# Eleven stores of decoded token weights move from ScalarE's DMA queue to SyncE's in a fused attention and two-mixer kernel

## The chip, the cores and the metric

The kernel runs on one core of one Trainium2 chip. The metric is the device time of one execution in microseconds (us). The kernel before was run three times; the median is 758.35 us, the runs lie between 756.17 and 761.12 us. Beside these stands one profiled execution, of which every row below is taken.

Engines are called as in the profile: PE is TensorE's matmul side and PEld its weight load, DVE is VectorE, ACT is ScalarE, POOL is GpSimd, SP is SyncE, which computes nothing and issues most of the DMAs. A name with a q (SPq, ACTq) is an engine's sequencer, which issues DMAs.

## The reference

Eight batches of 576 tokens, model width 512, all in float32. The steps, cut to what matters here:

```
kv  = einsum('bhsd,bhse->bhde', k, v);  out = einsum('bhsd,bhde->bhse', q, kv)
x   = out / sqrt(mean(out*out) + 1e-6) * g_norm           # heads side by side: (8, 576, 512)
gate = sigmoid(causal 5-tap depthwise conv of x);  val = x @ w_val
y   = (gate * val) @ w_out                                # end of the first stage
theta = y @ w_theta;  zr, zi = y*cos(theta), y*sin(theta)
u   = y + w_tok_r @ zr + w_tok_i @ zi                     # mixing over the tokens
result = u + relu(u @ w_ch)
```

Some weights arrive as 64-bit floats, two 32-bit words for each number, and the kernel turns them into float32 itself. w_tok_r and w_tok_i (called w_tok together) are 9 x 576 columns of 128 rows. They are needed only in the second stage, where u is made.

## The kernel before, in words

**Two stages.** The first stage (about the first 310 us) makes attention, the gated value product and w_out's product for one batch after the other, in a loop over i = 0..7 (line 392). It writes its result y of each batch to a DRAM buffer (`ydram`). The second stage (from line 445 on) reads y back, makes theta, the mixing over tokens and the channel product, and writes the result. Every product is done as three matmuls on a high part and a low part of each operand (`parts`, line 66: ACT copies the high part, DVE subtracts to get the low part).

**An iteration of the first stage.** PE makes the value products v of batch i, then w_out's products y of batch i, and between them the attention of batch i + 2: `key_value` (kvp, line 182), the products o with q (line 200), the sums of squares ss (line 212). DVE makes the gating (`acc`, line 288), the low parts (line 69), the convolution of the next batch (line 265), the inverse roots (lines 219 to 225) and the scaling of x by them (line 246). ACT makes high parts, squares, sigmoids (line 266) and the copies of y out of PSUM (yo, line 304), which it then stores itself on its own queue (`yd<-yo`, line 305).

**SP's queue in an iteration.** In the order of the trace: the inverse roots go to DRAM and come back broadcast (`rd<-y`, line 228, and two `yb<-rd`, line 233); then the next keys and values in eight loads (`kv`, lines 156 and 157), then the next q in four loads (line 168), then loads of raw weights (`raw_tk`, `raw_wt`, line 85).

**The decoding of chunks beside it.** Lines 430 to 441 run in iterations 1 to 6. Each of them takes one 512-wide chunk of w_theta (four in all) and three of w_tok (eleven in all, the last 64 wide). A chunk is loaded by SP (`fetch`, line 71, tile `raw_tk` or `raw_wt`, three buffers shared), decoded by four DVE operations and one of ACT (`decode`, line 88: DVE lines 94, 95, 96, ACT line 97, DVE line 98) into a tile `dst_tk` or `dst_wt`, **two buffers shared by both kinds**. A w_theta chunk is then split into parts that stay in SBUF (ACT line 112, DVE line 113). A w_tok chunk is stored to DRAM, into `tokdram` (`td<-dst_tk`, line 441), from where the second stage reads it (line 551). As the two buffers are shared, the first operation of a later chunk (line 94) must wait until the buffer's earlier content was read: by line 113, or by the DMA of line 441, until that has landed.

**What sets the order.** The text gives an order, but not the one that runs. A planner works out, before the run, the order of the instructions on each engine from estimated durations: at each time it takes, of the instructions whose inputs and buffers are there by its estimate, the one that stands first in urgency, and each engine then works off its list strictly in order. The block of lines 430 to 441 stands under `tc.high_priority(offset=-LATER)` with LATER = 1000, so that all of it, the loads, the decoding and the stores, counts as a thousand places less urgent than where it stands in the text. The waits are made from the data and buffers that are used. In iterations of the trace the chunks' decoding stands between the convolution's operations on DVE. [...]

**Names in the steps below.** The iteration of the trace that is called the third runs from the row `rd<-y` at 156.25 us to the one at 195.20 us, the fourth from there to 234.81 us, the fifth from there to 271.10 us, the second from 124.28 to 156.25 us. The f loads (line 330) are the first loads of the second stage; they go into the space that the raw and dst tiles had.

Of the kernel before, what the change touches and what calls it, by code (L numbers as in the profile page):

```python
# [43 lines left out]
def attention_moe_holo_kernel(ctx, tc, kvm, kvt, qt, gn, w_val, conv_w, w_out, w_th, w_tok, w_ch, outT):  # L44
# [5 lines left out]
    nc = tc.nc  # L50
# [37 lines left out]
    def decode(pool, raw, width, name, tag=""):  # L88

        if raw.dtype == F32:  # L90
            return raw
        dst = pool.tile([P, width if tag else DM], F32, tag="dst" + tag if pool is px else "fTt", bufs=(1 if tag else 2) if pool is px else 1, name=f"dst_{name}")[:, :width]
        lo, hi, d = raw[:, :width, 0], raw[:, :width, 1], dst.bitcast(I32)
        nc.vector.tensor_scalar(d, hi, 0x07FFFFFF, 3, ALU.bitwise_and, ALU.logical_shift_left)
        nc.vector.scalar_tensor_tensor(d, hi, -0x40000000, d, ALU.bitwise_and, ALU.bitwise_or)
        nc.vector.scalar_tensor_tensor(d, lo, 29, d, ALU.logical_shift_right, ALU.bitwise_or)
        nc.scalar.activation(hi.bitcast(F32), hi.bitcast(F32), AF.Square)
        nc.vector.scalar_tensor_tensor(dst, hi.bitcast(F32), TINY, dst, ALU.is_ge, ALU.mult)
        return dst
# [4 lines left out]
    def weight_chunk(pool, tiles, src, k, name, scale=None, raw=None):  # L104
        h, l = tiles
        if raw is None:
            raw = fetch(pool, src[:, k, :], DM, f"{name}_{k}")
        st = decode(pool, raw, DM, f"{name}_{k}")
        if scale is None:
            parts(h[:, k, :], l[:, k, :], st)  # L110
        else:
            nc.scalar.activation(h[:, k, :], st, AF.Copy, scale=scale)
            nc.vector.scalar_tensor_tensor(l[:, k, :], st, scale, h[:, k, :].bitcast(F32), ALU.mult, ALU.subtract)
# [14 lines left out]
    tokdram = dr.tile([P, 9 * S], F32, tag="td", name="td")  # L128
# [3 lines left out]
    px = px_stack.enter_context(tc.tile_pool(name="px", bufs=1, reuse_waits="tile", side="right"))  # L132
# [18 lines left out]
    def load_kv(b, pairs=range(NP)):  # L151
        kv = []
        for p in pairs:
            t = px.tile([P, 2, 5, P], F32, tag="kv", bufs=4, name=f"kv{b}_{p}")
            nc.gpsimd.memset(t[D:P, :, 4, :], 0.0)
            nc.sync.dma_start(out=t[:, :, 0:4, :], in_=kvm[b, p])
            nc.sync.dma_start(out=t[0:D, :, 4, :], in_=kvt[b, p])
            kv.append(t)
        return kv
# [11 lines left out]
    def key_value(b, kv):  # L171

        ps = one_bank(f"kvp{b}")
        for g in range(2):
            for e in range(2):
                es = slice(e * D, (e + 1) * D)
                at = slice((2 * g + e) * D, (2 * g + e + 1) * D)
                for c in range(5):
                    for j in range(2):

                        t = kv[2 * g + j]
                        nc.tensor.matmul(ps[j * D:(j + 1) * D, at], t[:, 0, c, es], t[:, 1, c, es],
                                         start=(c == 0), stop=(c == 4), tile_position=(0, j * D))
        kvs_of[b] = pa.tile([P, NP, D], F32, tag="kvs", bufs=2, name=f"kvs{b}")
        nc.scalar.activation(kvs_of[b], ps[:, 0:NP * D].rearrange("p (a e) -> p a e", e=D), AF.Copy)
# [92 lines left out]
    def value(b, x, xh, xl, sg, between):  # L278
        gh = pa.tile([P, NM, S], F32R, tag="gh", bufs=1, name=f"gh{b}")
        gl = pa.tile([P, NM, S], F32R, tag="gl", bufs=1, name=f"gl{b}")  # L280
        for m in range(NM):
            between(m)
            g = sg[m]
            ps = two_banks(f"v{b}_{m}")
            for h in range(2):
                product(ps[:, h], wv, m, xh, xl, h * HS)
            halves = lambda t: t.rearrange("p (h s) -> p h s", h=2)
            nc.vector.tensor_tensor(halves(g), ps, halves(g), ALU.mult)  # L288
            last, _ = parts(gh[:, m, :], gl[:, m, :], g)
            if m + EARLY < NM:  # L290
                sg.append(conv(b, m + EARLY, x))
        return gh, gl, last
# [34 lines left out]
    def load_y(b):  # L327
        f = qx.tile([P, NM, S], F32, tag="full", bufs=2, name=f"f{b}")
        for m in range(NM):
            nc.sync.dma_start(out=f[:, m, :], in_=ydram[b][:, m, :])  # L330
        for h in range(2):
            sl = slice(h * 256, (h + 1) * 256)
            to_tokens(sdram[b][sl, :], [(f[:, :, sl], (0, 256))], "fT", 2, f"fT{b}_{h}")
        yh = qx.tile([P, NM, DM], F32R, tag="yh", bufs=1, name=f"yh{b}")
        yl = qx.tile([P, NM, DM], F32R, tag="yl", bufs=1, name=f"yl{b}")
        for m in range(NM):
            parts(yh[:, m, :], yl[:, m, :], f[:, m, :DM])
        yt = qx.tile([P, 4, DM], F32, tag="yt", bufs=1, name=f"yt{b}")
        nc.sync.dma_start(out=yt, in_=sdram[b].rearrange("(c p) d -> p c d", p=P))
        return f, yh, yl, yt  # L340

    def load_tails(b):

        ft = qx.tile([P, NM, 2, D], F32, tag="ft", bufs=1, name=f"ft{b}")
        for j in range(2):
            nc.sync.dma_start(out=ft[:, :, j, :], in_=ydram[b + j][:, :, DM:S])
        to_tokens(stdram[b // 2], [(ft[:, :, j, :], (2 * j, D)) for j in range(2)], "fTt", 1, f"fTt{b}")
        th = qx.tile([P, NM, P], F32R, tag="th", bufs=1, name=f"th{b}")
        tl = qx.tile([P, NM, P], F32R, tag="tl", bufs=1, name=f"tl{b}")
        parts(th, tl, ft.rearrange("p m j s -> p m (j s)"))  # L350
        yts = []
        for j in range(2):
            t = qx.tile([P, S], F32, tag="tok", bufs=2, name=f"ytt{b}_{j}")[:, :DM]
            for r in range(2):
                nc.sync.dma_start(out=t[r * D:(r + 1) * D], in_=stdram[b // 2][j * D:(j + 1) * D, :])
            yts.append(t)
        return th, tl, yts
# [4 lines left out]
    raw = {}  # L362
# [29 lines left out]
    for i in range(B):  # L392
        if i == B - 1:
            px_stack.close()
            qx = ctx.enter_context(tc.tile_pool(name="qx", bufs=1, reuse_waits="tile", side="right"))
            ys = load_y(0)
            tls = load_tails(0)
            for k in range(CHFIRST):
                weight_chunk(qx, wch, w_ch, k, "wc")
        two = i + 2 < B  # L400
        if two:
            ahead = attention(i + 2, qs.pop(i + 2))

        def between(m):

            if two and m == 1:
                key_value(i + 2, kvs.pop(i + 2))
                if i + 3 < B:
                    kvs[i + 3] = load_kv(i + 3)
            if two and m == 3:  # L410
                next(ahead)

        gs = value(i, *xs, sg, between)
        if two:
            next(ahead)
            if i + 3 < B:
                qs[i + 3] = load_q(i + 3)
        if i + 1 < B:
            with tc.issue_after(gs[2].ins):
                *_, (nxs, last) = normalize(i + 1, *xy)  # L420
        if i == 0:
            for k in range(4):
                weight_chunk(px, wo, w_out, k, "wo", raw=raw[f"o{k}"])
        got = []
        first(i, *gs[:2], lambda: got.append(next(ahead) if two else None))
        xy = got[-1]
        if i + 1 < B:
            xs = nxs
            sg = [conv(i + 1, m, xs[0]) for m in range(EARLY)]
        if 1 <= i < B - 1:  # L430
            with tc.high_priority(offset=-LATER), tc.issue_after(last.ins):
                for _ in range(RATE[0]):
                    if todo:
                        w, src, k, name, scale = todo.pop(0)
                        weight_chunk(px, w, src, k, name, scale)
                for _ in range(RATE[1]):
                    if toks:
                        j = toks.pop(0)
                        sl = slice(j * DM, min((j + 1) * DM, 9 * S))
                        raw = fetch(px, w_tok[:, sl], sl.stop - sl.start, f"tk_{j}")  # L440
                        nc.scalar.dma_start(out=tokdram[:, sl], in_=decode(px, raw, sl.stop - sl.start, f"tk_{j}"))

# [111 lines left out]
    for b in range(B):  # L556
        f, zs = nxt
# [53 lines left out]
```

## Time and profile before

| | |
|---|---|
| median of 3 runs | 758.35 us (756.17 to 761.12) |
| time of the profiled execution | 757.05 us |
| its span, first to last instruction | 755.3 us |
| mean granted PE clock | 0.980 |
| DMA issues of line 441 | 11, 326 to 362 ns each on ACT's sequencer |
| from their issue to landing | 2.5 to 8.5 us, median 5.4 us |
| bytes of one such store | 256 KB (10 of them), 32 KB (the last) |
| DMA packets of ACT's queue, share of the 16 engines | 12.09 MB, 4.3% |
| DMA packets of SP's queue, share of the 16 engines | 89.75 MB, 42.3% |

The page of the profile gives, in this order: the busy time of each engine, the span in 40 slices, the DMA queues, the chain of work that ended last followed back from the last instruction, the groups of instructions, and the DMA issues. In the view of waits a row names the engine and line that waited, who released it, and then the sum in us, the number of times and the longest. In the view by windows each row is a stretch of the span: its length, then busy us and instruction count of each engine, the granted PE clock, the DMA share and GB/s. In the timeline a row begins with start and duration in us; brackets at the end hold the idle time before it and its releaser.

### The profile page before, as it was taken

How to read it: one execution, taken by the hardware profiler on the slowest of the kernel's cores; microseconds unless marked ns; L12 is line 12 of the kernel's file. 1: busy time of each engine (PE TensorE's matmuls, PEld its weight loads, DVE VectorE, ACT ScalarE, POOL GpSimd, SP SyncE). 2: the span in 40 equal slices, each digit the busy share in tenths (PEclk: the TensorE clock that was granted, in tenths of full speed). 3: DMA queues.
4: the chain of work that ended last, by engine and by line, in shares of the span. 5: the costliest groups of instructions: out<-in, count | busy, mean ns of one | idle time of the engine just before them, and what ended most of it. 6: DMA issues, size and time to landing. Idle time of an engine off the chain costs nothing.

```text
span 755.3 us, 14663 instructions
## 1 busy us (share of the span) xinstructions
PE 713.3 (94%) x6000; PEld 672.7 (89%) x6000; DVE 524.2 (69%) x930; ACT 337.6 (45%) x560; POOL 19.5 (3%) x72
## 2 busy tenths in 40 slices
PE   1679999998979899999999999999999999999998
PEld 1568989996969899889899899899999999998998
DVE  5389959978879999789883863853853934936504
ACT  2466565736364736376541641621732513614301
POOL 4000000000000000000000000000000000000000
PEclk9779999998989999999999999999999999999999
DMA  9949694978575257724336034063052160160101
GB/s 263 280 147 243 195 242 133 270 244 243 162 243 168 67 159 231 221 66 137 123 100 194 1 126 112 18 170 107 17 151 71 61 184 37 57 176 7 63 1 63
DMA packets 77058, 104.87 MB, mean 139 GB/s; under 512 B 11712, under 2 KB 42560, under 8 KB 76992
## 3 DMA queue, kind: packets, MB, share of 16 engines
q1 hardware_dynamic: 70224, 89.75, 42.3%
q10 hardware_dynamic: 6192, 12.09, 4.3%
q0 software_dynamic: 576, 2.10, 0.9%
q8 instruction: 47, 0.77, 0.4%
q14 instruction: 19, 0.16, 0.1%
HBM read 72.73 MB, written 31.19 MB: 138 GB/s over the span
## 4 chain that ended last, share of the span: by engine, by line
PE 64%; DVE 22%; ACT 6%; DMA 5%; issue 2%; SPq 0%; ACTq 0%; DVEq 0%
PE u L514 10%; PE u L512 10%; PE u L513 10%; DVE acc L265 9%; PE c L276 4%; PE c L275 4%; PE c L274 4%; PE th L460 3%; PE th L459 3%; PE th L458 3%; DMA td<-dst_tk 3%; DMA kv<-in_kvm_dram 2%; DVE xl L69 2%; DVE acc L288 2%; DVE gl L69 2%
## 5 line engine op out<-in xcount | busy, mean ns | idle before, releaser
L517 DVE TENSOR_TENSOR f<-u,f 128x288 f32<-128x288 f32 x64 | 26.5, 454 | 129.4 <-PE u L514 129.4
L265 DVE SCALAR_TENSOR_TENSOR acc<-x,cw,acc 128x576 f32<-128x576 f32 x128 | 101.9, 813 | 0.9 <-ACT acc L263 0.8
L68 ACT ACTIVATE uh<-f 128x288 fp32r<-128x288 f32 x64 | 26.2, 444 | 152.0 <-DVE f L517 152.0
L274 PE MATMUL y<-gh,woh 128*128 128x288 f32 x256 | 78.7, 308 | 2.9 <-DVE acc L288 1.7
L274 PE MATMUL v<-xh,wvh 128*128 128x288 f32 x256 | 77.7, 304 | 0.0
L276 PE MATMUL y<-gl,woh 128*128 128x288 f32 x256 | 76.8, 302 | 0.3 <-DVE gl L69 0.3
L275 PE MATMUL y<-gh,wol 128*128 128x288 f32 x256 | 77.0, 301 | 0.0
L276 PE MATMUL v<-xl,wvh 128*128 128x288 f32 x256 | 76.5, 299 | 0.0
L275 PE MATMUL v<-xh,wvl 128*128 128x288 f32 x256 | 76.1, 297 | 0.0
L274 PE MATMUL c<-uh,wch 128*128 128x288 f32 x256 | 75.4, 295 | 0.0
L276 PE MATMUL c<-ul,wch 128*128 128x288 f32 x256 | 75.4, 295 | 0.0
L275 PE MATMUL c<-uh,wcl 128*128 128x288 f32 x256 | 75.4, 294 | 0.0
L274 PEld LDWEIGHTS y<-gh,woh 128*128 128x128 f32 x256 | 49.9, 195 | 7.2 <-ACT x L205 3.1
L274 PEld LDWEIGHTS v<-xh,wvh 128*128 128x128 f32 x256 | 48.7, 190 | 3.9 <-issue 2.1
L460 PE MATMUL th<-wth,yl 128*128 128x512 f32 x128 | 50.3, 393 | 0.0
L459 PE MATMUL th<-wtl,yh 128*128 128x512 f32 x128 | 50.0, 391 | 0.0
L276 PEld LDWEIGHTS y<-gl,woh 128*128 128x128 f32 x256 | 49.6, 194 | 0.5 <-DVE gl L69 0.5
L458 PE MATMUL th<-wth,yh 128*128 128x512 f32 x128 | 50.0, 391 | 0.0
L275 PEld LDWEIGHTS y<-gh,wol 128*128 128x128 f32 x256 | 49.8, 195 | 0.0
L276 PEld LDWEIGHTS v<-xl,wvh 128*128 128x128 f32 x256 | 48.6, 190 | 0.3 <-issue 0.2
L275 PEld LDWEIGHTS v<-xh,wvl 128*128 128x128 f32 x256 | 48.8, 190 | 0.0
L275 PEld LDWEIGHTS c<-uh,wcl 128*128 128x128 f32 x256 | 48.0, 188 | 0.3
(188 smaller groups left out, 1946.4 us busy)
## 6 DMA issues: line engine op xcount, KB each, us to landing
kv<-in_kvm_dram SPq DMA_DIRECT2D x32, 512.0 KB, 9.1
q<-in_qt_dram SPq DMA_DIRECT2D x32, 288.0 KB, 7.0
yd<-yo ACTq DMA_DIRECT2D x32, 288.0 KB, 2.1
f<-yd SPq DMA_DIRECT2D x32, 288.0 KB, 4.0
out_dram<-f SPq DMA_DIRECT2D x64, 144.0 KB, 1.8
sd<-fT SPq DMA_DIRECT2D x64, 128.0 KB, 2.5
yt<-sd SPq DMA_DIRECT2D x8, 1024.0 KB, 5.4
yb<-rd SPq DMA_DIRECT2D x12, 576.0 KB, 7.0
```

What stands on the lines that cost most here:

```text
L69: return nc.vector.tensor_tensor(l, src, h.bitcast(F32), ALU.subtract), one
L265: nc.vector.scalar_tensor_tensor(a, x[:, m, k:k + S], cw[:, m * 5 + k:m * 5 + k + 1], a, ALU.mult, ALU.add)
L274: nc.tensor.matmul(ps, wh[:, m, ks], xh[:, k, tsl], start=(k == 0), stop=False)
L275: nc.tensor.matmul(ps, wl[:, m, ks], xh[:, k, tsl], start=False, stop=False)
L276: nc.tensor.matmul(ps, wh[:, m, ks], xl[:, k, tsl], start=False, stop=(k == 3))
L458: nc.tensor.matmul(ps, yh[:, k, :], wth[0][:, k, :], start=(k == 0), stop=False)
L459: nc.tensor.matmul(ps, yh[:, k, :], wth[1][:, k, :], start=False, stop=False)
L460: nc.tensor.matmul(ps, yl[:, k, :], wth[0][:, k, :], start=False, stop=(k == 3))
L512: nc.tensor.matmul(ps[:, :HS], zh[:, ms], wkh[:, j, sl], start=(i == 0), stop=False)
L513: nc.tensor.matmul(ps[:, :HS], zh[:, ms], wkl[:, j, sl], start=False, stop=False)
L514: nc.tensor.matmul(ps[:, :HS], zl[:, ms], wkh[:, j, sl], start=False, stop=(i == 8))
L517: nc.vector.tensor_tensor(f[:, m, sl], ps[:, :HS], f[:, m, sl], ALU.add)
```

## The change

Line 441 issues the store of a decoded w_tok chunk on SP's queue and not on ACT's. The stores of the w_out results (line 305) stay on ACT's queue. Nothing else is edited; the planner makes its order anew from the changed text.

```diff
                         raw = fetch(px, w_tok[:, sl], sl.stop - sl.start, f"tk_{j}")
-                        nc.scalar.dma_start(out=tokdram[:, sl], in_=decode(px, raw, sl.stop - sl.start, f"tk_{j}"))
+                        nc.sync.dma_start(out=tokdram[:, sl], in_=decode(px, raw, sl.stop - sl.start, f"tk_{j}"))
```

## The prediction

> **What bounds the kernel now.** I read the page first, for the whole and for the chain of work that ended last.
>
> ```profile
> span 755.3 us, 14663 instructions
> PE 713.3 (94%) x6000; PEld 672.7 (89%) x6000; DVE 524.2 (69%) x930; ACT 337.6 (45%) x560; POOL 19.5 (3%) x72
> PE u L514 10%; PE u L512 10%; PE u L513 10%; DVE acc L265 9%; PE c L276 4%; PE c L275 4%; PE c L274 4%; PE th L460 3%; PE th L459 3%; PE th L458 3%; DMA td<-dst_tk 3%; DMA kv<-in_kvm_dram 2%; DVE xl L69 2%; DVE acc L288 2%; DVE gl L69 2%
> ```
>
> PE fills 94% of the span, but the chain also holds 3% of the span, over 20 us, in the very stores that are moved. So the stores are not hidden. The chain in order of time says which of the eleven they are:
>
> ```profile
> 162.66 7.82 DMA td<-dst_tk
> ...
> 201.60 8.53 DMA td<-dst_tk
> ...
> 241.21 5.61 DMA td<-dst_tk
> ```
>
> Each took 5.6 to 8.5 us from issue to landing. Next the view by windows, cut at the five rows `rd<-y`, one row for each iteration from the second to the fifth (length, then busy us of PE, PEld, DVE, ACT, POOL):
>
> ```profile
> 124.28:156.25 31.97, 31.97 (x369) 29.92 (x368) 30.88 (x53) 19.50 (x31) 1.23 (x5) 1.00 0.84 237
> 156.25:195.20 38.95, 35.52 (x373) 32.06 (x373) 31.39 (x54) 20.82 (x34) 1.23 (x5) 0.91 0.74 220
> 195.20:234.81 39.61, 34.61 (x365) 31.89 (x365) 31.40 (x54) 20.29 (x32) 1.24 (x5) 0.91 0.67 204
> 234.81:271.10 36.29, 34.39 (x385) 31.87 (x384) 33.30 (x59) 21.34 (x33) 0.12 (x1) 1.00 0.38 112
> ```
>
> The second is filled by PE to the last hundredth of its 31.97 us. The third and fourth have the same DVE work within 2% (31.4 against 30.88 us), and last 7.0 and 7.6 us longer. What ends DVE's waits there:
>
> ```profile
> DVE dst_tk L94 <- DMA td<-dst_tk: 7.4, 2, 4.8
> DVE dst_wt L94 <- DMA td<-dst_tk: 5.5, 1, 5.5
> DVE dst_tk L98 <- ACT raw_tk L97: 1.7, 1, 1.7
> DVE wtl L113 <- ACT wth L112: 1.6, 1, 1.6
> ```
>
> Three waits for a store's landing, 4.8, 2.6 (7.4 less 4.8) and 5.5 us. The timeline of DVE shows the first:
>
> ```profile
> 170.50 0.43 DVE L94 TENSOR_SCALAR dst_tk<-raw_tk 128x512 int32<-128x512 int32 x1 [4.82 <-DMA td<-dst_tk]
> 170.84 0.75 DVE L69 TENSOR_TENSOR gl<-acc,gh 128x576 fp32r<-128x576 f32 x1
> 171.51 0.69 DVE L113 SCALAR_TENSOR_TENSOR wtl<-dst_wt,wth 128x512 fp32r<-128x512 f32 x1
> ```
>
> A decode of low urgency stands at the head of DVE's list, its buffer is still being stored, and the gating's low part (gl) behind it, which PE needs, stands still with it. PE then runs dry and gets half its clock for a while (the column after POOL is the granted clock):
>
> ```profile
> 170.00:175.00 5.00, 1.57 (x15) 0.41 (x17) 4.32 (x7) 2.04 (x4) 0.00 (x0) 0.81 0.74 220
> 175.00:180.00 5.00, 5.00 (x25) 4.13 (x26) 2.62 (x4) 3.51 (x7) 0.00 (x0) 0.51 0.88 211
> ```
>
> So in this stage DVE bounds, close to PE, and the ceiling of any cure of these stores is 7.0 + 7.6 us, for an iteration cannot go below PE's 32, and 2.6 us in the fifth: 17.2 us.
>
> **The change part by part.** *Off ACT.* Eleven issues leave ACT's sequencer.
>
> ```profile
> L441 ACTq DMA_DIRECT2D td<-dst_tk x11: 326/327/362, 134.9 to 280.6; - x11
> DMA to landing us min/median/max: 2.5/5.4/8.5
> ```
>
> 11 x 0.33 = 3.6 us of an engine that is busy for 19 to 21 of each 32 to 40 us. I cost this at 0. The cover is ACT's idle time; without it, it would be 3.6 us gained.
>
> *Onto SP: when the store is issued.* The trace cannot show this, since the order is planned anew. Ahead of it on SP stand, in the third iteration:
>
> ```profile
> 158.11 1.25 SPq L233 DMA_DIRECT2D yb<-rd  x2
> 159.47 0.57 SPq L156 DMA_DIRECT2D kv<-in_kvm_dram  x1
> ...
> 169.51 0.54 SPq L157 DMA_DIRECT2D kv<-in_kvt_dram  x1
> 174.10 3.31 SPq L168 DMA_DIRECT2D q<-in_qt_dram  x4
> 177.51 5.32 SPq L85 DMA_DIRECT2D raw_tk<-in_w_tok_dram  x2
> ```
>
> The store's data are ready at 162.62, when line 98 ends. One end: it is put there, between yb and kv. The other: it gives way to all the more urgent loads, the eight kv and four q. There is a nearest row: the raw loads belong to the same block of low urgency, and the first raw_tk at 177.51 needs the raw buffer that this same decode frees at 162.62. It was put behind kv and q all the same. The iteration before shows it too: a raw buffer is free after 129.6 (the last reading of raw_wt, row below), and the load into it stands at 144.42, behind q:
>
> ```profile
> L98 DVE SCALAR_TENSOR_TENSOR dst_wt<-raw_wt,dst_wt x1: 683/683/683, 129.6 to 129.6; 128x512 f32<-128x512 f32 x1
> ```
>
> ```profile
> 141.72 2.60 SPq L168 DMA_DIRECT2D q<-in_qt_dram  x4
> 144.42 0.53 SPq L85 DMA_DIRECT2D raw_tk<-in_w_tok_dram  x1
> ```
>
> So I take the far end: in the second to fourth iterations the stores go out behind q, just ahead of the raw loads, some 12 us after their data are ready.
>
> *What is late next.* With that, DVE's list cannot stay as it is. The q loads wait for PE's o, and o for the gating on DVE:
>
> ```profile
> SPq L168 <- PE o L200: 11.6, 6, 3.7
> ```
>
> ```profile
> PE o L200 <- DVE acc L288: 2.6, 1, 2.6
> ```
>
> and that gating stands behind the waiting line 94. A store behind q, with line 94 waiting for it ahead of the gating, would be a circle, which a planner that works in time never makes. It must give the later decode another place: a buffer is free as soon as line 113 has read the w_theta chunk (171.51, one operation behind gl), without any store. So line 94 moves a few operations back in the third iteration. In the fourth, two w_tok chunks fill both buffers and their stores go out behind q; the w_theta chunk that follows them (the 5.5 us wait) moves back to the next iteration, by when they have landed. Either way DVE no longer stands before a store.
>
> *The sum.* The second iteration is the model: 31.97 us at 30.88 of DVE. The third and fourth have 31.4, so 32.5; I leave 1.0 for the waits on ACT of 1.7 and 1.6 us above, partly kept, and get 33.5 each. 38.95 - 33.5 = 5.4 and 39.61 - 33.5 = 6.1 us gained. In the fifth there are no kv and q loads; the store stands right behind yb, the chunks are as many, the wait of 2.6 us may go or stay: 0 to 2.6, I take 0.5, for the store still follows yb closely. Lost: a chunk that moves back costs DVE its decoding later (0.43 + four of 0.69 = 3.2 us), and it ends in the sixth iteration, ahead of the f loads, which already wait for the last decode:
>
> ```profile
> SPq L330 <- DVE dst_tk L98: 5.3, 1, 5.3
> ```
>
> 0 to 3.6 us, with the last store's own 0.33 issued ahead of them. As the decoding is only moved and missing where it stood, I take 1.0. In sum 5.4 + 6.1 + 0.5 - 1.0 = 11.0 us less. The profiled execution took 757.05 us, 1.3 below the median of 758.35; the forecast against the median is 747.4 us. Its own range: from the ceiling, 17.2 less, 741.2, to half of it, 753.
>
> *The transfer itself.* [...] Rows of the loads that SP issued at 159.47, and at 160.09 and 160.83:
>
> ```profile
> L156 SPq DMA_DIRECT2D kv<-in_kvm_dram x1: 570/570/570, 159.5 to 159.5; - x1
> DMA to landing us min/median/max: 10.0/10.0/10.0
> ```
>
> ```profile
> DMA to landing us min/median/max: 10.2/10.6/10.9
> ```
>
> They land at 169.5, 170.3 and 171.8; the store, issued on its own queue at 162.66, lands at 170.48, after loads issued up to 2.6 us before it and 1.3 us ahead of the one issued 1.8 us before. [...]
>
> **The rivals.** *A: the store is put ahead of the kv loads.* SP then waits from 159.4 to 162.6 for line 98, and the kv loads behind it start 3.2 us later, which nobody feels: they serve the next iteration. The store has only yb ahead of it:
>
> ```profile
> L233 SPq DMA_DIRECT2D yb<-rd x2: 593/600/608, 158.1 to 158.8; - x2
> DMA to landing us min/median/max: 5.6/6.8/8.0
> ```
>
> The second yb lands at 158.76 + 8.0 = 166.7, the store about 1 us later (the distance between the store and the load before it above, 170.48 - 169.5), 167.7 in place of 170.5: 2.8 us. The fourth likewise, by these rows:
>
> ```profile
> L233 SPq DMA_DIRECT2D yb<-rd x2: 593/600/608, 197.1 to 197.8; - x2
> DMA to landing us min/median/max: 5.7/7.0/8.2
> ```
>
> 197.8 + 8.2 + 1 = 207.0 in place of 201.60 + 8.53 = 210.1: 3.1. In the fifth, where a store comes behind yb as it is, I take 0.4. Sum 6.3, 752.0 us. For it: line 98 ends before SP's kv rows in time. Against it: the place of the raw loads.
>
> *B, the other side: the store goes behind the kv loads but ahead of q, and DVE's list stays.* No circle then. The store is issued after 169.51 + 0.54 = 170.05 and lands behind the last kv (169.51 + 5.8 = 175.3), at 176.3 in place of 170.5: line 94 waits 5.8 us more. The same again in the fourth: 11.6 us slower, 770.0. It decides from the point where the plan takes the store to land before line 94 though kv stands ahead of it: any landing later than 170.5 loses. For it: the plan before already had line 94 too early by 4.8 us. Against it: the same plan puts raw loads behind q as well, not between.
>
> *C: the gain is given back.* SP's loads also wait for stores that they have no data in common with, once for 4.0 us in the second iteration:
>
> ```profile
> SPq L157 <- DMA td<-dst_tk: 4.0, 1, 4.0
> ```
>
> Three such waits ahead of loads that are needed soon, or the late chunks ahead of the f loads, give back 11 to 12 us, and the first stage ends as late as now: 758. [...] Against C: the waits of 4.8 and 5.5 us are on the chain, and a store that is issued at another time changes them.
>
> **How the numbers follow.** The forecast, 747.4 us, has a chance of 0.5; A 0.17, B 0.17, C 0.16. About 1% (7.6 us) is what a measurement of this kernel can tell from no change: below 750.8 is faster, above 765.9 slower. Faster takes 0.42 of the forecast's 0.5 and 0.07 of A and C, so 0.49; slower 0.15 of B; the same 0.36. The range from 741 (the ceiling) to 762 holds the forecast, A and C, and leaves out B and little else. The forecast's own range is 741 to 753.
>
> **What would show it.** Right: on SP `td<-dst_tk` rows between q and raw_tk in the second to fourth iterations; no DVE wait on td of over 1 us in them; iterations of 33 to 34 us; PE's granted clock 1.00 from 160 to 230 us. A shows in td rows between yb and kv and waits of 2 us that remain. B shows in waits of line 94 of about 10 us. The forecast is wrong if the waits on td go and the first stage does not end earlier; then the f loads' wait for line 98 has grown.

## The result, and the profile after

The kernel after takes 749.8 us (median of 4 runs, 746.98 to 749.87) against 759.58 us for the kernel before (median of 4, the three runs named ahead and one more, 756.17 to 761.12): 9.8 us less, a ratio of 0.9868 with a 95% interval of 0.9825 to 0.9912. The forecast of 747.4 us stood for 11.0 less than 758.35. The profiled execution of after took 749.74 us, 7.3 less than that of before.

The page of after:

```profile
span 748.0 us, 14663 instructions
PE 710.6 (95%) x6000; PEld 671.4 (90%) x6000; DVE 524.4 (70%) x930; ACT 336.8 (45%) x560; POOL 19.4 (3%) x72
PE u L514 10%; PE u L512 10%; PE u L513 10%; DVE acc L265 10%; PE c L276 5%; PE c L274 5%; PE c L275 5%; PE th L460 3%; PE th L458 3%; PE th L459 3%; DMA kv<-in_kvm_dram 3%; DVE xl L69 2%; DVE acc L288 2%; DVE gl L69 1%; ACT x L205 1%
```

The 3% of the chain that lay in `td<-dst_tk` are gone, and DVE has no wait on a store left at all. The view by windows, again cut at the rows `rd<-y`, second to fifth iteration:

```profile
128.62:160.57 31.95, 31.95 (x369) 29.90 (x368) 30.86 (x53) 20.04 (x31) 1.24 (x5) 1.00 0.86 244
160.57:194.50 33.93, 33.93 (x418) 31.72 (x419) 31.39 (x54) 20.28 (x32) 1.23 (x5) 1.00 0.83 242
194.50:225.68 31.18, 30.68 (x328) 28.32 (x323) 28.56 (x49) 18.81 (x29) 1.23 (x5) 1.00 0.85 239
225.68:259.55 33.87, 33.86 (x383) 31.74 (x382) 33.52 (x59) 21.32 (x33) 0.12 (x1) 1.00 0.47 144
```

38.95, 39.61 and 36.29 us have become 33.93, 31.18 and 33.87, and the granted clock, 0.91 before in two of them, is 1.00. The third is now filled by PE to the last hundredth, with 418 matmuls for 373 before, and the fourth has 328 for 365. So a part of what the fourth gained is only where the cut falls; the two together last 65.11 us for 78.56. The timeline of SP in the third iteration shows where the stores stand:

```profile
171.74 0.54 SPq L157 DMA_DIRECT2D kv<-in_kvt_dram  x1
175.34 2.60 SPq L168 DMA_DIRECT2D q<-in_qt_dram  x4
178.03 1.02 SPq L441 DMA_DIRECT2D td<-dst_tk  x2
181.61 2.74 SPq L85 DMA_DIRECT2D raw_tk<-in_w_tok_dram  x2
```

Behind q, just ahead of the raw loads; the second and fourth iterations look the same. And the timeline of DVE there:

```profile
170.15 0.76 DVE L69 TENSOR_TENSOR gl<-acc,gh 128x576 fp32r<-128x576 f32 x1 [0.15 <-ACT gh L68]
170.83 0.68 DVE L113 SCALAR_TENSOR_TENSOR wtl<-dst_wt,wth 128x512 fp32r<-128x512 f32 x1
171.43 0.75 DVE L288 TENSOR_TENSOR acc<-v,acc 128x576 f32<-128x576 f32 x1
172.10 0.41 DVE L94 TENSOR_SCALAR dst_tk<-raw_tk 128x512 int32<-128x512 int32 x1
```

Line 94 stood ahead of gl and waited 4.82 us. Now it stands behind gl, line 113 and the next gating, and starts at once, while the earlier chunk's store has not even been issued (178.03). The w_theta chunk of the fourth iteration has moved to the start of the fifth:

```profile
226.30 0.43 DVE L94 TENSOR_SCALAR dst_wt<-raw_wt 128x512 int32<-128x512 int32 x1
```

**What was given back.** From the sixth `rd<-y` to the end the kernel before took 755.3 - 271.10 = 484.2 us; after takes 748.0 - 259.55 = 488.45, that is 4.25 more. DVE's timeline after the fifth iteration shows it:

```profile
273.52 2.62 DVE L246 TENSOR_TENSOR x<-x,yb 128x1152 f32<-128x1152 f32 x2
276.17 2.63 DVE L69 TENSOR_TENSOR xl<-x,xh 128x1152 fp32r<-128x1152 f32 x2
278.72 0.22 DVE L98 SCALAR_TENSOR_TENSOR dst_tk<-raw_tk,dst_tk 128x64 f32<-128x64 f32 x1
...
287.21 2.37 DVE L321 STREAM_TRANSPOSE fT<-f 128x1024 f32<-128x1024 f32 x2 [1.65 <-DMA f<-yd]
```

and the kernel before at the same point:

```profile
280.37 0.23 DVE L98 SCALAR_TENSOR_TENSOR dst_tk<-raw_tk,dst_tk 128x64 f32<-128x64 f32 x1
...
283.85 2.62 DVE L246 TENSOR_TENSOR x<-x,yb 128x1152 f32<-128x1152 f32 x2
...
295.81 2.36 DVE L321 STREAM_TRANSPOSE fT<-f 128x1024 f32<-128x1024 f32 x2
```

The last decode now stands behind the scaling of x and its low parts. On SP the last store waits 7.5 us for it, and the f loads stand behind that store:

```profile
271.40 7.89 SPq L441 DMA_DIRECT2D td<-dst_tk  x2
279.38 2.52 SPq L330 DMA_DIRECT2D f<-yd  x4
```

DVE waits 1.65 us for the f loads. DVE is late from there on, PE waits 2.50 us for the last gating of the stage (1.7 before) and has less clock in the next 5 us:

```profile
301.09 0.61 PE L274 MATMUL y<-gh,woh 128*128 128x288 f32 x1 [2.50 <-DVE acc L288]
```

```profile
300.00:305.00 5.00, 3.91 (x19) 3.91 (x20) 3.99 (x6) 1.80 (x4) 0.00 (x0) 0.66 0.89 339
```

Before had no such stretch there: its clock is 1.00 in every 5 us from 275 to 350 us. In the 90 us about this point PE waits 5.8 us in all for 3.3 before, 2.5 more. The stretch costs, as an estimate from its row, 0.34 of 5 us, which is 1.7. Together that is 4.2 of the 4.25.

**The account.** The three iterations gain 5.02 + 8.43 + 2.42 = 15.9 us, the end gives back 4.25. That is 11.6 us from the second `rd<-y` on (755.3 - 124.28 = 631.0 against 748.0 - 128.62 = 619.4). In the profiled executions 4.3 us of it do not show, because the second `rd<-y` came at 128.62 and not at 124.28 us, a stretch in which the change touches nothing. Of these, 2.8 us lie ahead of the first `rd<-y` (94.89 for 92.09 us). The first loads of keys landed 2.9 us later there, by the chain of before and then that of after:

```profile
8.77 9.81 DMA kv<-in_kvm_dram
```

```profile
9.56 11.93 DMA kv<-in_kvm_dram
```

The eleven experiments below have the same work up to this point, but for e3 and e8 (three buffers) and the three that begin the decoding early; their second `rd<-y` lies between 124.2 and 129.3 us. So the stretches are compared from there. One execution each of e2, e3 and e11 was far slower, with a lower mean granted clock (870.6, 784.47 and 996.01 us at 0.758, 0.846 and 0.661), and is left out of the medians and ratios below.

### The profile page after: what moved, and what is told of

The parts are those of the page before. It is cut to its first block, busy times and chain, and to the rows that moved or that the text cites. A ratio compares the mean times of both kernels' runs of the same rounds, so it can differ in the third digit from the quotient of the medians.

```text
span 748.0 us, 14663 instructions
## 1 busy us (share of the span) xinstructions
PE 710.6 (95%) x6000; PEld 671.4 (90%) x6000; DVE 524.4 (70%) x930; ACT 336.8 (45%) x560; POOL 19.4 (3%) x72
## 4 chain that ended last, share of the span: by engine, by line
PE 61%; DVE 25%; DMA 6%; ACT 5%; issue 2%; SPq 0%; ACTq 0%; DVEq 0%
PE u L514 10%; PE u L512 10%; PE u L513 10%; DVE acc L265 10%; PE c L276 5%; PE c L274 5%; PE c L275 5%; PE th L460 3%; PE th L458 3%; PE th L459 3%; DMA kv<-in_kvm_dram 3%; DVE xl L69 2%; DVE acc L288 2%; DVE gl L69 1%; ACT x L205 1%
```

## The experiments

The theory, **"order"**: the gain comes from the place of line 94 on DVE. A decode may not stand ahead of urgent work while its buffer is still being stored; the queue of the store matters only in that it makes the planner move that decode. The rival, **"queue"**: it comes from leaving ACT's queue. In the table, "end" runs from the sixth `rd<-y` to the end of the span. Ratios are to runs of the kernel before beside each.

| kernel | median us | ratio (95%) | third | fourth | fifth | end |
|---|---|---|---|---|---|---|
| before | 759.58 | 1 | 38.95 | 39.61 | 36.29 | 484.2 |
| after | 749.8 | 0.9868 (0.9825 to 0.9912) | 33.93 | 31.18 | 33.87 | 488.5 |
| e1 DVE's order as after, stores on ACT | 750.22 | 0.9876 (0.9842 to 0.9910) | 37.44 | 31.33 | 34.71 | 486.0 |
| e2 stores on POOL | 760.80 | 1.0012 (0.9993 to 1.0031) | 39.32 | 39.51 | 39.41 | 484.5 |
| e3 three buffers, stores on ACT | 743.29 | 0.9783 (0.9745 to 0.9820) | 32.11 | 33.48 | 35.14 | 484.2 |
| e4 stores on SP ahead of or between kv | 748.23 | 0.9842 (0.9810 to 0.9873) | 33.95 | 33.35 | 34.27 | 485.2 |
| e5 one store on SP | 755.95 | 0.9946 (0.9922 to 0.9969) | 33.93 | 39.79 | 39.32 | 484.2 |
| e6 two stores on SP | 751.17 | 0.9880 (0.9853 to 0.9906) | 39.10 | 31.59 | 35.34 | 485.9 |
| e7 after, last two chunks swapped | 745.21 | 0.9794 (0.9760 to 0.9828) | 33.93 | 31.18 | 33.87 | 486.7 |
| e8 three buffers, stores on SP | 745.31 | 0.9808 (0.9781 to 0.9836) | 32.10 | 33.80 | 34.95 | 484.9 |
| e9 after, begun an iteration earlier | 741.31 | 0.9768 (0.9741 to 0.9796) | 31.17 | 32.19 | 34.06 | 482.7 |
| e10 three buffers, ACT, earlier | 741.48 | 0.9766 (0.9736 to 0.9796) | 33.47 | 32.66 | 31.75 | 483.9 |
| e11 before, begun an iteration earlier | 760.44 | 1.0019 (1.0004 to 1.0034) | 38.82 | 37.55 | 33.11 | 483.7 |

**e1: the order alone, without the queue.** The block of line 430 is written so that DVE's list becomes nearly that of after, by order edges on DVE, while line 441 stays on ACT:

```diff
-        if 1 <= i < B - 1:
-            with tc.high_priority(offset=-LATER), tc.issue_after(last.ins):
+        if 1 <= i < B - 1 and i != 3:
+            with tc.high_priority(offset=-LATER):
+                for c in {4: (3, 4)}.get(i, (i,)):
+                    anchor = gs[2] if c == 3 else last
...
+                            with tc.issue_after(anchor.ins):
+                                behind = weight_chunk(px, w, src, k, name, scale)
...
+                            with tc.issue_after((behind if c == 2 else anchor).ins):
+                                st = decode(px, raw, sl.stop - sl.start, f"tk_{j}")
                             nc.scalar.dma_start(out=tokdram[:, sl], in_=st)
```

(`behind` is line 113 of the block's w_theta chunk, `gs[2]` the last low part of the following iteration's gating.)

> The stores stay on ACT's queue as in the kernel before; only the order of the decoding on DVE is written as the kernel after has it (third iteration: line 94 of the later w_tok chunk behind line 113; the block of the fourth iteration's w_theta chunk begins in the fifth). Theory 'order' (the gain comes from line 94 no longer standing at the head of DVE's list while its buffer is being stored, whichever queue stores it): no wait on td over 1 us in the third and fourth iterations, these 31 to 34 us long, time 747 to 752 us, like the kernel after. [...]

750.22 us, as after, with every store on ACT. From the second `rd<-y` on it takes 621.4 us, for 619.4 in after and 631.0 before. That the medians agree to 0.4 us is in part luck: the third iteration is 3.5 us longer than in after, the end 2.5 shorter. The third iteration is a miss. By the timeline of DVE:

```profile
167.30 0.69 DVE L113 SCALAR_TENSOR_TENSOR wtl<-dst_wt,wth 128x512 fp32r<-128x512 f32 x1
171.60 0.43 DVE L94 TENSOR_SCALAR dst_tk<-raw_tk 128x512 int32<-128x512 int32 x1 [3.62 <-DMA td<-dst_tk]
171.95 0.75 DVE L288 TENSOR_TENSOR acc<-v,acc 128x576 f32<-128x576 f32 x1
```

Line 94 stands behind line 113, which has just freed a buffer, and still waits 3.62 us for a store: with the store on ACT's queue, the planner gives the chunk the buffer of that store. So the moved store settles not only the place of line 94 but also which buffer it takes. The fourth iteration, where order is all, does what was expected: 31.33 us.

**e2: the queue alone, without the order.**

```diff
-                        nc.scalar.dma_start(out=tokdram[:, sl], in_=decode(px, raw, sl.stop - sl.start, f"tk_{j}"))
+                        nc.gpsimd.dma_start(out=tokdram[:, sl], in_=decode(px, raw, sl.stop - sl.start, f"tk_{j}"))
```

> The stores leave ACT's queue for POOL's, while in the third to fifth iterations the order on DVE stays that of the kernel before (line 94 ahead of the gating's low part). Theory 'order': the waits on td stay at 4 to 8 us each, the third and fourth iterations stay at 38 to 41 us, time 755 to 765 us. Rival 'queue': ACT is relieved just as in the kernel after, so 747 to 752 us.

760.80 us: nothing gained, with ACT as relieved as in the kernel after. DVE's three waits are those of before, the one in the fifth iteration twice as long:

```profile
DVE dst_tk L94 <- DMA td<-dst_tk: 10.5, 2, 5.3
DVE dst_wt L94 <- DMA td<-dst_tk: 5.4, 1, 5.4
```

e1 and e2 together decide against the rival: the gain comes without leaving ACT's queue, and leaving it does not bring the gain. Whether SP's queue by itself helps, e3 and e8 tell.

**e3 and e8: a third buffer, on either queue.**

```diff
-bufs=(1 if tag else 2) if pool is px else 1, name=f"dst_{name}")
+bufs=(1 if tag else 3) if pool is px else 1, name=f"dst_{name}")
```

> The kernel before with three buffers for decoded chunks in place of two, stores on ACT's queue. Theory 'order', in its more general form 'a decode may not stand before a store that is under way': with a third buffer no line 94 meets such a store, third and fourth iterations of 32 to 34 us, time 743 to 751 us. Rival 'queue': 755 to 761 us, since ACT issues the same eleven stores at the same places.

> The kernel after with three buffers for decoded chunks. Theory 'order': once no decode stands before a store under way, the queue is of no weight: 742 to 747 us, within 3 us of the third buffer with stores on ACT's queue, and the last part no longer than there. Rival 'queue': SP's queue brings its 9 to 10 us also here, 733 to 737 us. A further rival: the stores behind q hold two of three buffers, and waits on td of 2 us or more come back, 748 to 752 us.

743.29 us with the stores left on ACT, 745.31 with them on SP; the intervals of the two ratios overlap, so SP's queue by itself brings nothing that shows. The windows of e3 for the third and fourth iterations:

```profile
158.47:190.58 32.11, 32.11 (x370) 30.06 (x370) 31.12 (x54) 19.16 (x31) 1.23 (x5) 1.00 0.85 246
190.58:224.06 33.48, 33.44 (x399) 31.16 (x400) 30.36 (x53) 21.12 (x33) 1.24 (x5) 1.00 0.85 246
```

The third is filled by PE to the last hundredth, with line 94 early and the store where it was. What was missing in the kernel before was a buffer. One wait of line 94 on a store is left, 1.2 us in the fifth, where none was expected. No late decode either: its end is that of before, 484.2 us.

**e4: the stores on SP, ahead of kv.**

```diff
-                        nc.sync.dma_start(out=tokdram[:, sl], in_=decode(px, raw, sl.stop - sl.start, f"tk_{j}"))
+                        st = decode(px, raw, sl.stop - sl.start, f"tk_{j}")
+                        with tc.high_priority(offset=2 * LATER):
+                            nc.sync.dma_start(out=tokdram[:, sl], in_=st)
```

> The kernel after with its stores given a higher urgency, so that SP issues them ahead of or between the kv loads of the same iteration and not behind q; line 94 of the later chunk still stands behind the gating that it blocked before. Theory 'order': the place on SP is of no weight as long as line 94 stands late, so 745 to 752 us, within 3 us of the kernel after. Rival A of the prediction: 752 us with waits on td of about 2 us that remain. Rival 'SP is held up' (kv and q loads come later as SP waits for line 98): 753 to 760 us.

748.23 us. SP's timeline in the third iteration:

```profile
159.75 1.27 SPq L233 DMA_DIRECT2D yb<-rd  x2
164.29 0.33 SPq L443 DMA_DIRECT2D td<-dst_tk  x1
164.73 0.57 SPq L156 DMA_DIRECT2D kv<-in_kvm_dram  x1
```

The place on SP is rival A's, the time is not. Here too the planner has moved line 94 behind the gating, and the waits on td that remain are 1.7 and 0.5 us. The kv loads start 3.6 us later after `rd<-y` than in the kernel before (6.85 for 3.22), which costs nothing that shows.

**e5 and e6: one part of the change alone.**

```diff
+(nc.sync if j == 2 else nc.scalar).dma_start(...      # e5
+(nc.sync if j in (4, 5) else nc.scalar).dma_start(... # e6
```

> Only one of the eleven stores goes out on SP, that of the third w_tok chunk (j = 2), which the third iteration's line 94 waited for; the other ten stay on ACT. On DVE only the line 94 of the next w_tok chunk moves behind the gating's low part, line 113 and the next gating. Theory 'order': the third iteration falls from about 39 to 34 us, the fourth keeps 39 to 40 us and its wait of 5 us, time 753 to 756 us, half of the gain. Rival 'queue': one store of eleven brings a tenth of the gain, 758 to 759 us.

> Only the stores of the fifth and sixth w_tok chunks (j = 4, 5), of the fourth iteration, go out on SP; the other nine stay on ACT. Theory 'order': the w_theta chunk of the fourth iteration moves to the fifth, the third iteration keeps its 39 us, the fourth falls to 31 to 34 us, the fifth to 34 to 36, and a late last decode takes back 1 to 4 us at the f loads: time 750 to 755 us. Rival 'queue': 757 to 758 us.

One store of eleven brings the third iteration to 33.93 us, two bring the fourth to 31.59, and in each the other iteration stays at 39 to 40. By the ratios the parts are worth 0.54 and 1.20%, 1.74% together, against 1.32% (0.88 to 1.75) for the change. The give-back accounts for much of the difference: the end is 1.7 us longer than before in e6, 4.25 in after, and 2.5 us are 0.3%. In e5 the fifth lasts 39.32 us: its wait on a store is 5.7 us long. In e2 that wait was over 5 too. Line 94 stands there in both as in the kernel before, in whose profiled execution the wait was 2.6. So the fifth iteration of before probably varies by some 3 us between executions, and its 2.4 us of gain would be a low reading; with one trace of before, that is not shown.

**e7: the given-back part.** The kernel after with its last two chunks in the other order:

```diff
-    toks = list(range(11))
+    toks = list(range(9)) + [10, 9]
```

> The kernel after with its last two w_tok chunks decoded in the other order (the 64-wide one first), so that the last line 98 stands ahead of the scaling of x in the sixth iteration, not behind it and the low parts. Nothing else moves. Theory 'give-back': the kernel after loses about 4 us in the sixth iteration as its f loads wait for that line 98; here the f loads go out 5 to 7 us earlier, DVE doesn't wait for them, the stretch from the sixth rd to the end shortens by 2 to 4.5 us, time 745 to 748 us. Rival 'the 4 us are lost elsewhere': f loads earlier, time unchanged at 749 to 751 us.

745.21 us. That is 4.6 us less than after by the medians, but the profiled executions differ by only 1.7 us from the second `rd<-y` on (617.7 for 619.4), and by 3.7 in when that row comes (124.95 for 128.62 us), which the edit does not touch. So the time inside 745 to 748 is in part luck. The last line 98 now stands ahead of line 246, and DVE has no wait ahead of fT:

```profile
268.11 0.68 DVE L98 SCALAR_TENSOR_TENSOR dst_tk<-raw_tk,dst_tk 128x512 f32<-128x512 f32 x1
...
269.69 2.62 DVE L246 TENSOR_TENSOR x<-x,yb 128x1152 f32<-128x1152 f32 x2
...
281.64 2.37 DVE L321 STREAM_TRANSPOSE fT<-f 128x1024 f32<-128x1024 f32 x2
```

The f loads come 6.5 us earlier after the sixth `rd<-y`, as expected. The end falls from 488.45 to 486.7 us: 1.75 us, just under the 2 to 4.5 expected, and about the 1.65 us that DVE waited. The other 2.5 stay, so the f loads are not the whole of it. PE still waits 2.4 us for the last gating, and the granted clock falls behind it as in after:

```profile
295.00:300.00 5.00, 4.48 (x23) 4.48 (x24) 3.47 (x6) 2.05 (x3) 0.00 (x0) 0.66 0.71 234
```

As an estimate from this row, that is 1.7 of the 2.5 us.

**e9, e10, e11: the block an iteration earlier,** in the first one, where DVE has 8 us idle (24.15 busy of 32.19 in the kernel before):

```diff
-        if 1 <= i < B - 1:
+        if i < B - 1:
```

> The kernel after with the block of loads, decoding and stores begun one iteration earlier (in iterations 0 to 6 of the loop, not 1 to 6), where DVE has 8 us of each 32 idle. So the last chunks are decoded in the fourth and fifth iteration of the trace and nothing of them is left in the sixth. Theory 'give-back': the stretch from the sixth rd to the end falls from 488.5 us (kernel after) to 483 to 485 us, the fifth iteration to 32 to 33 us: 742 to 746 us. Rival 'lost elsewhere': the first iterations, which fill PE already, grow by DVE's new work and the time stays at 748 to 752 us.

> Stores on ACT's queue, three buffers for decoded chunks, and the block begun one iteration earlier. Theory 'order': with neither a decode ahead of a store under way nor a late decode, all of the third to fifth iterations come to 32 to 33 us and the last part stays at 484 us: 739 to 743 us, the fastest of all, with the stores where the kernel before had them. Rival 'queue': no better than the kernel after, 747 to 751 us.

> The kernel before with the block begun one iteration earlier, two buffers, stores on ACT's queue. Theory 'order': the waits of line 94 on td only move an iteration forward, 4 to 6 us each, and two or three iterations still last 38 to 40 us: 754 to 760 us, while the same edit with the stores on SP is 8 us or more faster. Rival 'the waits depended on the iteration': 744 to 750 us.

e9 (the kernel after with this edit) takes 741.31 us, just under its range, e10 (three buffers, ACT) 741.48, both faster than before and after; e11 (the kernel before with it) 760.44, just over its range. The last two rows of iterations, of e9 and then of e10:

```profile
191.01:223.20 32.19, 32.19 (x370) 30.07 (x370) 31.12 (x54) 19.51 (x31) 1.24 (x5) 1.00 0.87 246
223.20:257.26 34.06, 34.06 (x385) 32.01 (x385) 32.08 (x58) 20.70 (x34) 0.12 (x1) 1.00 0.34 104
```

```profile
190.63:223.29 32.66, 31.63 (x350) 29.18 (x346) 31.14 (x54) 19.59 (x30) 1.23 (x5) 1.00 0.82 241
223.29:255.04 31.75, 31.71 (x367) 29.75 (x367) 29.57 (x54) 19.87 (x32) 0.12 (x1) 1.00 0.32 96
```

With no decode left in the sixth iteration the end is 482.7 and 483.9 us: the whole give-back is gone, and with it the stretch at the lower clock (1.00 over the 45 us from the sixth `rd<-y` on, in both). So what e7 left goes when no decoding is late. How much of it was DVE's work and how much the clock is not shown: e4 has a pause of 2.42 us there and keeps its clock, with an end of 485.2. Of e9's 8.5 us against after by the medians, 5.3 show from the second `rd<-y` on; the second iteration, where more is decoded now, lasts 33.94 us for 31.95. That the fifth of e9 would come to 32 to 33 us was a miss (34.06, all of it PE), and the third of e10 is 33.47. e11 keeps the waits, an iteration earlier, and its second iteration lasts 38.74 us:

```profile
DVE dst_tk L94 <- DMA td<-dst_tk: 10.2, 2, 5.6
DVE dst_wt L94 <- DMA td<-dst_tk: 4.7, 1, 4.7
```

e9 and e11 differ in text in nothing but the queue of line 441: 19.1 us. e9 and e10 differ in queue and buffers, and by 0.2 us. The same edit is worth 19.1, 9.8 or, once the buffer is there (e3 and e8), nothing that shows.

## Why the prediction was right

**The place of the stores: right.** Behind q, ahead of raw_tk, in the second to fourth iterations, as argued from the place of the raw loads.

**The planner must move line 94: right, and the cause.** The third iteration's line 94 went three operations back, behind line 113; the fourth's w_theta chunk went to the fifth. e1 and e2 show that this moves the time and the queue by itself does not. e3 shows that the same is to be had without either.

**The sizes.** Third: 33.93 us for 33.5 forecast, a gain of 5.0 for 5.4. That it came so close is luck: the 33.5 were DVE's work and part of two waits on ACT, and what fills the 33.93 us is PE. Fourth: 31.18 for 33.5, a gain of 8.4 for 6.1; the term took 31.4 us of DVE work as before, though the step ahead of it had moved a chunk out, and its DVE row is 28.56. It also shows that PE's 32 us, from which the ceiling was taken, are no floor for an iteration as it is cut here. Fifth: 2.4 for 0.5; the wait of 2.6 went altogether.

**The loss: the mis-sized term.** 1.0 us was taken, 3.6 was its upper end, 4.25 it is. The direction and the place (the last decode ahead of the f loads) were right. What was missed: the last line 98 can fall behind the 5.3 us of lines 246 and 69, the decoding that is late costs DVE in the one iteration whose end nobody covers, and the pause of PE there, 2.50 us, was followed by a stretch at a granted clock of 0.66, 1.7 us by estimate. e7 removes 1.75, e9 all of it. The four errors nearly cancel, which is luck: 15.9 - 4.25 = 11.6 for 12.0 - 1.0 = 11.0. By the medians the gain was 9.8; how much of the difference is the start of each execution can't be told, since only one execution of each kernel has a trace. The upper end of the forecast's range, 753, fits half of the 11.0; half of the ceiling of 17.2, as the text reads, would give 749.7.

**The terms at nothing: right.** ACT's 3.6 us of issue brought nothing (e2, 760.80 us). Stores of 6.4 to 8.2 us to landing in the second to fourth iterations cost next to nothing. DVE does not wait for them. SP's `rd<-y` does, though it has no data in common with them:

```profile
SPq L228 <- DMA td<-dst_tk: 4.5, 3, 1.7
```

ACT's copies yo wait for them 1.4 us in all. But PE is idle for only 0.5 us of these three iterations.

**Rival A** had its place tried in e4. It came out 3.8 us faster than its 752 us; rival A had reckoned with DVE's list as it was, and in e4 line 94 stands further back. Its transfer price, a landing 1 us after the second yb, stays an estimate: what the trace of e4 gives is 3.9 us from issue to landing as the median of the two stores from 160 to 180 us. **Rival B** needed the store ahead of q and DVE's list unchanged; neither came about. **Rival C** had a true part: the late chunk did give back 4.25 us at the f loads, but not 11. Its waits of SP on stores came too, on `rd<-y`, but cost next to nothing. The queue alone brought nothing: with a third buffer, ACT and SP lie 2.0 us apart with overlapping intervals (e3, 743.29 us, and e8, 745.31), and on POOL's queue nothing is gained (e2, 760.80 us). What another queue brought here was another place in an order.

"Wrong if the first stage does not end earlier" is not met: the last store of y (line 305) goes out at 314.5 us for 321.9. The f loads come only 1.2 us earlier by the clock of the span (279.38 for 280.62), but 5.6 us earlier counted from the second `rd<-y` (150.76 for 156.34).

## What to carry to other kernels

When work of low urgency waits and holds up what stands behind it on its engine, as line 94 did for 4.82 us here, ask first which buffer it waits for: one more buffer was worth as much here as moving the stores, and more. When a change moves a DMA to another queue under a planner, work out what the planner can no longer place where it stood; the transfer itself may be of no weight, as here at 6.4 to 8.2 us to landing. And work that is pushed back ends up somewhere: look at the last iteration, where nothing covered it here (4.25 us).

## What the runs showed of the hardware

A store of 256 KB issued at the same point, behind the same loads, took as long on a third queue as on the second: 7.82 us from ACT in the kernel before, 7.94 from POOL in e2 (its chain of waits):

```profile
163.52 7.94 DMA td<-dst_tk
```

On SP ahead of or between the kv loads the two stores of the third iteration took 3.9 us in the median (e4), and behind q those of the second to fourth took 6.4 to 8.2 (after).

The start of an execution varies with nothing changed: the second `rd<-y` comes between 124.2 and 129.3 us, along with PE's wait for the first keys (15.2 us in e6, 18.9 in e5). That is half of the gain that was to be measured.

A pause of PE of nearly the same length was charged differently: 2.4 us at the last gating in e7 was followed by a stretch at a granted clock of 0.66 (the row shown there), 2.42 us at the same place in e4 by none:

```profile
300.00:305.00 5.00, 5.00 (x40) 4.97 (x39) 3.46 (x6) 1.37 (x2) 0.00 (x0) 1.00 0.36 100
```

What sets the two apart the runs do not show.
